# Second-half projections by token block, attention copies on one queue, GpSimd normalising twelve tiles, and a new bank order, in a fused attention and gated-linear block

## The chip, the cores and the metric

The kernel runs on one core of one Trainium2 chip. The metric is device time in microseconds (us), lower is better. Engine names in the profile: PE is TensorE (PEld its weight loads), DVE is VectorE, ACT is ScalarE, POOL is GpSimd, SP is SyncE; a "q" after the name is that engine's instruction queue when it issues DMAs.

## The reference

For 2048 tokens of width 640, in bfloat16:

```python
xn = layernorm(x)                                   # no scale, no bias
q, k, v = split(xn @ wqkv)                          # 32 heads of 20
logits[s, w] = q[s] . k[s - 2*w] * 20**-0.5         # w = 0..7, masked where s - 2*w < 0
attn = softmax(logits) ; o[s] = sum_w attn[s, w] * v[s - 2*w]
h = (xn @ w_gate) * (xn @ w_up)                     # width 1536
out = x + o @ wo + h @ w_down
```

## The kernel before

A small scheduler records every operation in program order, finds its dependencies and emits the semaphore waits. Each engine runs its own operations in the order in which they were recorded, so an operation placed behind a late one is late too.

Layer norm works by tile of 128 tokens, 16 tiles. DVE makes statistics, ACT takes the square root of the variance, DVE inverts it and normalises. Tiles 0 to 3 are transposed by PE; tiles 4 to 15 by a DMA issued from SP.

```python
op("dve", lambda e: e.reciprocal(rstd, sd), r=[("sd", t)], w=[("rstd", t)], name=f"rstd{t}")
op("dve", lambda e: e.tensor_scalar(xs, x, mv[:, 0:1], rstd, op0=ALU.subtract, op1=ALU.mult),
   r=[x, mv, ("rstd", t)], w=[xs], name=f"lnap{t}")
if t >= NTP:                                        # NTP = 4
    op("sp", lambda e: e.dma_start_transpose(o, xs), r=[xs], w=[o], dma=True, name=f"xT{t}")
```

Q and K of the first 1024 tokens are projected while the layer norm runs. Then GpSimd copies the last 14 columns of K's first half in front of its second half (the seam), and the second half's projections begin, in blocks of 512 tokens (`j`): block 2 is tiles 8 to 11, block 3 is tiles 12 to 15.

```python
def k_seam():
    op("pool", lambda e: e.tensor_copy(o, i), r=[i], w=[o], name="kseam")
# ... cut ...
for i, (m, j, which) in enumerate([(m, j, which) for m in range(NCH) for j in (2, 3) for which in (0, 1)]):
    fill.append((1.08, lambda which=which, m=m, j=j: proj(which, m, j)))
# ... cut: then V, gate/up groups and down/out groups, woven with DVE's attention steps
```

Each projection group is five matmuls into one PSUM bank, which ACT evicts; six banks rotate here. DVE forms the logit products in SBUF (q times shifted k), does most of the softmax and the weighted sum of v. The attention weights are spread over partitions by 16 DMAs for each half of the tokens:

```python
for q in range(NSB):
    for r in range(4):
        dma(dst, src, ..., eng=("sp", "act")[r % 2], group=("atb", h))
```

## Time and profile before

| | before |
|---|---|
| time at the start | 267.09 us, median of 3 (266.22 to 267.16) |
| profiled span | 265.8 us |
| PE busy | 256.7 us, 97% |
| DVE busy | 215.7 us, 81% |
| GpSimd busy | 5.3 us |
| PE's granted clock | full throughout, in this execution |

The share of busy time does not tell what a change is worth; PE's waits do. These are lines of the timeline of the kernel before, PE only: start, length, engine, line, operation, count, and in brackets the idle time ahead of the piece and what ended it. The last line is from a later stretch.

```profile
15.95 4.38 PE L436 MATMUL PS<-XNT,WQKV 128*128 128x128 bf16 x75 [0.48 <-ACT KH L450]
20.17 11.08 PE L443 MATMUL PS<-XNT,WQKV 128*128 128x256 bf16 x100
31.09 2.32 PE L423 MATMUL PS<-XNT,WQKV 128*128 128x512 bf16 x10
35.20 1.06 PE L423 MATMUL PS<-XNT,WQKV 128*128 128x512 bf16 x4 [1.79 <-DMA XNT<-XNS]
...
103.68 1.25 PE L576 MATMUL PS<-XNT,WG 128*128 128x512 bf16 x5 [3.26 <-ACT HT L578]
```

PE loses 0.48 us to a bank, 1.8 us to the transpose of tile 15, and 3.3 us to an eviction. The last one has its cause on ACT, of which these are timeline lines:

```profile
93.98 9.00 ACTq L283 DMA_DIRECT2D ATB<-LOG  x8
103.03 0.60 ACT L578 ACTIVATE HT<-PS 128x512 bf16<-128x512 f32 x1 [8.45 <-issue]
```

ACT's queue spends 9.0 us on issuing eight attention copies, and evicts nothing meanwhile; PE runs out of banks.

DVE's own load in the layer norm, one tile's worth, and the seam copy beside the first product (timeline, DVE and POOL; the "waits for" of the copy's 31 us is only its being early):

```profile
30.46 0.45 DVE L370 TENSOR_SCALAR XNS<-XST,MV,SD 128x640 bf16<-128x640 bf16 x1
...
33.91 3.36 DVE L466 TENSOR_TENSOR SL<-QH,KH 128x6144 f16<-128x6144 bf16 x1 [1.36 <-ACT KH L450]
33.94 3.43 POOL L454 COPY KH<-KH 128x70 bf16<-128x70 bf16 x1 [31.45 <-ACT KH L450]
```

A copy of 70 elements a partition takes 3.43 us beside a DVE product of 3.36 us.

### The profile page before, as it was taken

The numbers are of one execution on the slowest core, as the hardware profiler recorded it, in microseconds if no ns is written. First come the engines' busy times: TensorE is split into PE (matmuls) and PEld (weight loads), VectorE is DVE, ScalarE is ACT, GpSimd is POOL, SyncE is SP. The second block draws the span as 40 slices with busy tenths as digits, with TensorE's granted clock in tenths as the row PEclk, the third lists the DMA queues.
The fourth block names the chain that finished last, engine by engine and source line by source line (L and its number), as shares of the span: only waits on it lengthen the run. The fifth ranks groups of instructions, "written<-read, shape, count | busy, mean of one in ns | idle before, by whom it ended". The sixth has DMA issues, their size and how long they took to land.

```text
span 265.8 us, 4020 instructions
## 1 busy us (share of the span) xinstructions
PE 256.7 (97%) x1669; PEld 151.2 (57%) x1669; DVE 215.7 (81%) x240; ACT 106.1 (40%) x193; POOL 5.3 (2%) x13
## 2 busy tenths in 40 slices
PE   8999979999999995999999999999999999999996
PEld 3899835455554442444457754446774444777775
DVE  5799889999985992999997897999999999722211
ACT  3565557555557514655560004752003555100000
POOL 2000050000000000000000000000000000000000
PEclk9999999999999999999999999999999999999999
DMA  6959689200000078009101189100113000031301
GB/s 197 322 131 148 122 257 403 83 2 0 0 0 2 0 157 232 3 7 357 57 0 49 52 175 206 36 2 0 49 52 100 0 0 2 4 94 52 99 27 49
DMA packets 21922, 23.46 MB, mean 88 GB/s; under 512 B 9872, under 2 KB 19472, under 8 KB 21904
## 3 DMA queue, kind: packets, MB, share of 16 engines
q1 hardware_dynamic: 20992, 20.95, 27.7%
q10 hardware_dynamic: 912, 2.26, 4.1%
q8 instruction: 13, 0.21, 0.3%
q14 instruction: 5, 0.04, 0.0%
HBM read 14.42 MB, written 2.62 MB: 64 GB/s over the span
## 4 chain that ended last, share of the span: by engine, by line
PE 82%; DVE 8%; ACTq 3%; DMA 3%; SPq 2%; issue 1%; ACT 1%
PE PS L576 37%; PE PS L607 28%; PE PS L423 16%; ACTq L283 3%; DVE XNS L370 2%; PE PS L484 2%; SPq L283 2%; DVE STATS L354 2%; DMA XST<-in_A_x_dram 2%; DVE STATS L348 2%; DMA XNT<-XNS 1%; DVE MV L360 1%; DVE SD L369 1%; ACT HT L578 0%; ACT USX L578 0%
## 5 line engine op out<-in xcount | busy, mean ns | idle before, releaser
L576 PE MATMUL PS<-XNT,WG 128*128 128x512 bf16 x240 | 59.7, 379 | 3.3 <-ACT HT L578 3.3
L576 PE MATMUL PS<-XNT,WU 128*128 128x512 bf16 x240 | 59.6, 379 | 0.0
L607 PE MATMUL PS<-WD,HT 128*128 128x320 bf16 (+1 forms) x396 | 57.6, 295 | 0.0
L578 ACT ACTIVATE HT<-PS 128x512 bf16<-128x512 f32 x48 | 29.1, 606 | 68.0 <-PE PS L576 34.5
L607 PEld LDWEIGHTS PS<-WD,HT 128*128 128x128 bf16 x396 | 38.1, 98 | 14.7
L423 PE MATMUL PS<-XNT,WQKV 128*128 128x512 bf16 x200 | 43.9, 379 | 1.8 <-DMA XNT<-XNS 1.8
L550 DVE TENSOR_TENSOR PVB<-VO,ATB 128x10240 f16<-128x10240 bf16 x8 | 43.9, 5486 | 0.1
L576 PEld LDWEIGHTS PS<-XNT,WG 128*128 128x128 bf16 x240 | 23.3, 98 | 31.7 <-ACT HT L578 3.8
L576 PEld LDWEIGHTS PS<-XNT,WU 128*128 128x128 bf16 x240 | 23.4, 98 | 28.5 <-issue 0.4
L611 DVE TENSOR_TENSOR FOUT<-PS,XR 128x320 bf16<-128x320 f32 (+1 forms) x33 | 15.5, 476 | 29.1 <-PE PS L607 29.1
L578 ACT ACTIVATE USX<-PS 128x512 bf16<-128x512 f32 x48 | 29.0, 605 | 17.7 <-PE PS L576 17.2
L423 PEld LDWEIGHTS PS<-XNT,WQKV 128*128 128x128 bf16 x200 | 23.3, 118 | 22.0 <-DMA XNT<-XNS 2.3
L545 DVE TENSOR_TENSOR PVB<-PVB 128x5120 f16<-128x5120 f16 (+1 forms) x16 | 34.4, 2148 | 0.0
L466 DVE TENSOR_TENSOR SL<-QH,KH 128x6144 f16<-128x6144 bf16 x8 | 26.8, 3352 | 1.4 <-ACT KH L450 1.4
L581 DVE TENSOR_TENSOR HT<-HT,USX 128x512 bf16<-128x512 bf16 x48 | 18.7, 416 | 10.9 <-ACT USX L578 10.9
L607 PE MATMUL PS<-WO,VO 128*128 128x320 bf16 (+1 forms) x165 | 27.1, 295 | 0.0
L607 PEld LDWEIGHTS PS<-WO,VO 128*128 128x128 bf16 x165 | 15.9, 98 | 5.9
L474 DVE TENSOR_TENSOR SL<-SL,TMP 128x4096 f16<-128x4096 f16 x8 | 18.3, 2289 | 0.2
L466 DVE TENSOR_TENSOR TMP<-QH,KH 128x4096 f16<-128x4096 bf16 x8 | 18.4, 2300 | 0.0
L429 ACT ACTIVATE VO<-PS 128x512 bf16<-128x512 f32 x20 | 11.9, 597 | 9.8 <-PE PS L423 9.8
L436 PE MATMUL PS<-XNT,WQKV 128*128 128x128 bf16 x200 | 12.7, 220 | 0.7 <-ACT KH L450 0.5
L436 PEld LDWEIGHTS PS<-XNT,WQKV 128*128 128x128 bf16 x200 | 11.6, 118 | 1.9 <-ACT KH L450 0.6
(49 smaller groups left out, 138.0 us busy)
## 6 DMA issues: line engine op xcount, KB each, us to landing
XR<-in_A_x_dram SPq DMA_DIRECT2D x16, 160.0 KB, 2.3
XST<-in_A_x_dram SPq DMA_DIRECT2D x15, 160.0 KB, 4.0
out_dram<-FOUT SPq DMA_DIRECT2D x15, 160.0 KB, 1.8
ATB<-LOG SPq DMA_DIRECT2D x16, 128.0 KB, 4.9
ATB<-LOG ACTq DMA_DIRECT2D x16, 128.0 KB, 5.0
WG<-in_B_w_gate_dram SPq DMA_DIRECT2D x1, 1920.0 KB, 9.9
WU<-in_B_w_up_dram SPq DMA_DIRECT2D x1, 1920.0 KB, 14.1
WD<-in_B_w_down_dram SPq DMA_DIRECT2D x1, 1920.0 KB, 8.3
```

The lines of the kernel that those rows point to most:

```text
L283: return op(eng, lambda e: e.dma_start(o, i), r=r, w=w, dma=True, name=name, group=group)
L423: op("pe", (lambda l, x, c: lambda e: e.matmul(PS[:, b, :], l, x, start=(c == 0), stop=(c == NCH - 1)))(l, x, c), r=[l, x], w=[PS[:, b, :] ...
L436: op("pe", (lambda o, l, x, st, sp: lambda e: e.matmul(o, l, x, start=st, stop=sp))(o, l, x, st, sp), r=[l, x], w=[o], name=f"pp{which}_{m ...
L466: return lambda: op("dve", lambda e: e.tensor_tensor(o[:], qw, kw, ALU.mult), r=[q, k], w=[o[:]], name=f"prod{h}_{p}_{c0}")
L474: lambda: op("dve", lambda e: e.tensor_tensor(a, a, b, ALU.add), r=[a, b], w=[a], name=f"psum{h}_{p}")),
L545: return lambda: op("dve", lambda e: e.tensor_tensor(o, x, y, ALU.add), r=[x, y], w=[o], name=f"{name}_{b}")
L550: lambda: op("dve", lambda e: e.tensor_tensor(PVB[:], vw, aw, ALU.mult), r=[v, a], w=[PVB[:]], name=f"pv_{b}")),
L576: op("pe", (lambda l, x, c: lambda e: e.matmul(PS[:, b, :], l, x, start=(c == 0), stop=(c == NCH - 1)))(l, x, c), r=[l, x], w=[PS[:, b, :] ...
L578: op("act", lambda e: e.activation(o, PS[:, b, :], ACT.Copy), r=[PS[:, b, :]], w=[o], name=f"guev{which}_{m}_{j}")
L581: h_pending.append(lambda: op("dve", lambda e: e.tensor_tensor(h, h, o, ALU.mult), r=[h, o], w=[h], name=f"h{m}_{j}"))
L607: op("pe", (lambda l, x, i, b: lambda e: e.matmul(PS[:, b, 0:wid], l, x, start=(i == 0), stop=(i == n - 1)))(l, x, i, b), r=[l, x], w=[PS[ ...
L611: op("dve", (lambda o, xr, b: lambda e: e.tensor_tensor(o, PS[:, b, 0:wid], xr, ALU.add))(o, xr, b), r=[PS[:, b, :], xr], w=[o], name=f"fi ...
```

## The change

The intent: ask for the late tiles later, keep DMA issues off ACT, remove the bank wait, and take 0.45 us a tile off DVE by letting GpSimd normalise. The core of the diff:

```diff
-        op("dve", lambda e: e.tensor_scalar(xs, x, mv[:, 0:1], rstd, op0=ALU.subtract, op1=ALU.mult),
+        op("dve" if t < NTP else "pool",
+           lambda e: e.tensor_scalar(xs, x, mv[:, 0:1], rstd, op0=ALU.subtract, op1=ALU.mult),
 ...
-        for q in range(NSB):
-            for r in range(4):
+        for r in range(4):
+            for q in range(NSB):
                 src, dst = LOG[h][32 * q:32 * q + 32], ATB[h][r:128:4, q]
-                dma(dst, src, ..., eng=("sp", "act")[r % 2], group=("atb", h))
+                dma(dst, src, ..., group=("atb", h))
 ...
-    h_keep = [1]
+    h_keep = [3]
 ...
+        if t0 == 2:
+            bank_ring[:] = [5, 6, 0, 7, 2, 3, 4, 1]
 ...
-    bank_ring[:0] = [6, 7]
 ...
-[(m, j, which) for m in range(NCH) for j in (2, 3) for which in (0, 1)]
+[(m, j, which) for j in (2, 3) for m in range(NCH) for which in (0, 1)]
```

Cut here: the place where the loads of the down and out weights are recorded, and two start constants of the weaving (PE 30.6 to 31.0, DVE 31.5 to 31.8).

More of the change, by code (lines that the diff above doesn't have):

```diff
@@ L529, in attn_move @@
     def attn_move(h):
-        for q in range(NSB):
-            for r in range(4):
+        for r in range(4):
+            for q in range(NSB):
                 src, dst = LOG[h][32 * q:32 * q + 32], ATB[h][r:128:4, q]
-                dma(dst, src, r=[src], w=[dst], name=f"atb{h}_{q}_{r}", eng=("sp", "act")[r % 2], group=("atb", h))
+                dma(dst, src, r=[src], w=[dst], name=f"atb{h}_{q}_{r}", group=("atb", h))
     def pv_steps(b):
@@ L699, in exp_preload @@
         op("act", lambda e: e.activation(DUM[:, 0:1], EPSC[:, 0:1], ACT.Exp), r=[EPSC[:]], w=[DUM[:]], name="exp_preload")
-    t_pe, t_dve = [30.6], [31.5]
+    t_pe, t_dve = [31.0], [31.8]
     fill, pos = [], [0]
@@ L704, in build_kernel @@
     batches = []
-    for i, (m, j, which) in enumerate([(m, j, which) for m in range(NCH) for j in (2, 3) for which in (0, 1)]):
+    loaded = []
+    for i, (m, j, which) in enumerate([(m, j, which) for j in (2, 3) for m in range(NCH) for which in (0, 1)]):
         fill.append((1.08, lambda which=which, m=m, j=j: proj(which, m, j)))
@@ L738, in take @@
         t_pe[0] = max(t_pe[0], at) + 0.44 + 0.2175 * NKC * len(batch)
+        if h == 1 and batch[-1][0] == 3:
+            down_loads()
+            out_loads()
+            loaded.append(True)
     def run_fill(until, upto=None):
@@ L746, in run_fill @@
             if it[0] == "dn":
-                if pv_done[0] <= it[1]:
+                if pv_done[0] <= it[1] or not loaded:
                     return
@@ L813, in build_kernel @@
     settle()
-    down_loads()
-    out_loads()
     for it in headB:
```

## The prediction

> What bounds it now. The page gives TensorE (PE) 97% busy and 82% of the chain that ended last. In the timeline, second-half PE work runs back to back: 40 projection groups and 96 gate/up groups start every 1.08 us, 32 down/out groups every 2.31 us, four logit batches cost about 1.5 us each. That sums to about 227 us, and it occupies 31.1 to 263.5 us (232.4 us): about 5.4 us is stall, in two gaps. VectorE (DVE, 81%) finishes its last attention step at 230 us, well ahead of PE.
>
> The stalls (timeline):
> 1. At 33.2 us PE waits 1.95 us for the transpose of token tile 15. Layer norm on DVE runs 1.65 us a tile, its last normalise ends at 32.6 us, and a transpose lands 2.7 us after issue. The old order needs it in the third group.
> 2. At 100.3 us PE waits 3.4 us. ScalarE's queue issues eight attention copies for 9.0 us, so evictions stop and the PSUM banks run out.
> 3. At 15.5 us PE waits 0.48 us for a bank: tile 3's first projection group takes the bank of the previous pair's mixed group before it is evicted.
>
> What the change does.
> - Token-block order: tiles 12 to 15 are needed only after ten groups (10.8 us), so about 41 us; stall 1 goes: -1.95 us.
> - All 32 copies on SyncE: no DMA issue on ScalarE; stall 2 goes: -3.4 us. Sixteen copies at 0.86 us take about 14 us of SyncE, plus 5 us to land; with row-outer order the first quarter is complete only with copy 13. The DVE has two logit pairs (16 us) and several gate products before it reads them, so this should just fit.
> - Bank order: removes stall 3, at most -0.48 us.
> - GpSimd normalises 12 tiles: DVE loses 0.45 us a tile, its chain falls to about 1.2 us a tile, so ScalarE's evictions no longer wait for late variances and the first logit product should start near 31.5 us instead of 33.9. The Trainium skill, GPSIMD Engine Reference, section 3.1, gives 1.03 cycles an element for short bodies at 1.2 GHz; my estimate from it is 0.7 to 1.3 us for 640 elements. No run shows it yet. The same page says GpSimd shares its SBUF interface with DVE instructions that read two SBUF inputs; this trace agrees: the 70-element seam copy took 3.43 us beside a 3.36 us DVE product. In the layer norm DVE runs one-input operations, so I expect no blocking there. Tile 5 may land about 0.5 us later, which could eat the gain of the bank order.
> - Three gate products kept back: fewer DVE waits for up evictions (10.9 us now); PE hardly gains. Down-weight loads: no effect.
>
> Sum: -5.0 to -5.9 us on a PE-bound chain, minus small new waits. Predicted 261.6 us, 8 in 10 between 260.4 and 263.2. Chances: faster by over 2% 0.52, within 2% 0.45, slower 0.03.
>
> What would show it right: no PE gap near 33 us and 100 us; no DMA issue on ScalarE after start; GpSimd normalises at 0.7 to 1.3 us; second-half projections starting at 30.6 to 31.1 us; span about 260 us.
>
> What would make it wrong: GpSimd above about 1.6 us a tile, so tile 11 or the seam copy comes late and, once DVE products start, is blocked behind them; ScalarE held by the seam copy until PE runs out of banks; attention copies so late on one queue that the products lag and down/out groups wait; delayed gate products blocking an up eviction.

## The result, and the profile after

| | before | after |
|---|---|---|
| time, same rounds | 267.12 us, median of 4 (266.22 to 268.76) | 285.83 us, median of 4 (285.56 to 286.69) |
| ratio of fast runs | | 1.070, 95% interval 1.064 to 1.076 |
| span | 265.8 us | 285.0 us |
| GpSimd busy | 5.3 us | 48.1 us |
| mean granted clock of PE | 1.00 | 0.964 |

Here and below a ratio is the mean time of one kernel's fast runs over that of the kernel before in the same rounds, so it is not quite the ratio of the medians quoted.

The change is 7% slower. First the page's line for the new GpSimd work in the changed kernel (busy us, mean ns of one, idle before it), and that operation's own view (shortest, median, longest in ns):

```profile
L371 POOL TENSOR_SCALAR XNS<-XST,MV,SD 128x640 bf16<-128x640 bf16 x12 | 45.7, 3825 | 10.9 <-DVE SD L369 10.9
```

```profile
L371 POOL TENSOR_SCALAR XNS<-XST,MV,SD x12: 2499/2500/8206, 13.4 to 50.9; 128x640 bf16<-128x640 bf16 x12
```

The median is 2.50 us, and the longest 8.2 us. DVE did the same operation in 0.45 us. Now PE in the changed kernel (timeline), the counterpart of the lines of before:

```profile
21.47 12.78 PE L444 MATMUL PS<-XNT,WQKV 128*128 128x256 bf16 x100 [2.23 <-DMA XNT<-XNS]
36.27 7.50 PE L424 MATMUL PS<-XNT,WQKV 128*128 128x512 bf16 x34 [2.03 <-issue]
60.51 5.87 PE L424 MATMUL PS<-XNT,WQKV 128*128 128x512 bf16 x14 [16.73 <-ACT KH L430]
```

Three new waits stand there. The first, 2.23 us, is for the transpose of an early tile. The second is labelled "issue", but the times say what it is: twelve operations run back to back from 13.43 us, so the eighth, which is tile 11, ends at 13.43 + 8 x 2.485 = 33.3 us, and its transpose lands about 2.7 us later, at 36.0 us, which is when PE begins with block 2. The third is 16.7 us for an eviction into K. The view of ACT's waits, the DVE and POOL timelines of that stretch, and the operation on GpSimd that ended it:

```profile
ACT KH L430 <- POOL KH L455: 21.9, 1, 21.9
```

```profile
34.91 3.36 DVE L467 TENSOR_TENSOR SL<-QH,KH 128x6144 f16<-128x6144 bf16 x1 [3.75 <-ACT KH L451]
38.19 2.28 DVE L467 TENSOR_TENSOR TMP<-QH,KH 128x4096 f16<-128x4096 bf16 x1
40.51 2.77 DVE L475 TENSOR_TENSOR SL<-SL,TMP 128x4096 f16<-128x4096 f16 x1
...
35.77 7.00 POOL L371 TENSOR_SCALAR XNS<-XST,MV,SD 128x640 bf16<-128x640 bf16 x1
42.75 8.21 POOL L371 TENSOR_SCALAR XNS<-XST,MV,SD 128x640 bf16<-128x640 bf16 x1
50.94 8.20 POOL L371 TENSOR_SCALAR XNS<-XST,MV,SD 128x640 bf16<-128x640 bf16 x1
59.10 0.66 POOL L455 COPY KH<-KH 128x70 bf16<-128x70 bf16 x1
```

ACT waited 21.9 us for the seam copy, which stood on GpSimd's queue behind the normalises of tiles 13, 14 and 15. Those three took 7.0, 8.2 and 8.2 us, because DVE's products had begun. One DVE round of two products and a sum takes 8.2 us, and exactly one normalise ends in each round. Since ACT is in order, it could not evict anything, and PE, which had filled its six banks, stopped from 43.8 to 60.5 us.

Then PE's clock. Lines of the table by stretch of the changed kernel (stretch in us, length, busy time and count of PE, PEld, DVE, ACT, POOL, granted clock, DMA share, GB/s):

```profile
60.00:62.00 2.00, 1.50 (x4) 0.60 (x5) 0.00 (x0) 1.98 (x5) 0.00 (x0) 0.50 0.58 96
64.00:66.00 2.00, 2.00 (x7) 0.65 (x5) 0.00 (x0) 1.49 (x3) 0.00 (x0) 0.51 1.04 402
66.00:68.00 2.00, 1.95 (x10) 1.11 (x10) 0.00 (x0) 0.89 (x2) 0.00 (x0) 1.00 1.02 404
```

After the long stop PE runs at half clock until about 66 us. The Trainium skill, page "TensorE: Matmul & The Clock Gate", Part 1, says that PE falls to half clock after an idle window of about 3.4 us and returns after about as long a busy one. This trace agrees that a stop costs more than its length: PE worked at half clock from 60.5 to 65.9 us, which is, as my estimate, 2.7 us lost. It does not agree on the idle time that this takes: the clock had also halved from 21.6 to 24.8 us, after a wait of only 2.23 us.

Where the time went, by the start of each stage in the two timelines:

| stage begins | before | after | later by |
|---|---|---|---|
| second-half projections | 31.09 | 36.27 | 5.2 |
| gate/up groups | 79.31 | 101.88 | 22.6 |
| down/out groups | 137.58 | 156.71 | 19.1 |
| last addition | 263.52 | 282.64 | 19.1 |

The 5.2 us came from the late tiles up to 11: block 2 begins when tile 11 has landed, so the first wait and a clock halved from 21.6 to 24.8 us after it only ate time in which PE would have waited anyway. (In the seam-on-ScalarE run below the clock stayed full there, and block 2 still begins at 36.34 us.) In the next stage 17.4 us came: the 16.7 us stop and about 2.7 us of half clock, less the 1.8 us wait that the new order did remove. The stage after gives back 3.5 us, the wait behind ACT's DMA issues. From there on nothing changes.

### The profile page after: what moved, and what is told of

The parts are those of the page before. It is cut to its first block, busy times and chain, and to the rows that moved or that the text cites. A ratio compares the mean times of both kernels' runs of the same rounds, so it can differ in the third digit from the quotient of the medians.

```text
span 285.0 us, 4001 instructions
## 1 busy us (share of the span) xinstructions
PE 259.1 (91%) x1652; PEld 152.0 (53%) x1669; DVE 212.2 (74%) x228; ACT 108.3 (38%) x193; POOL 48.1 (17%) x25
## 4 chain that ended last, share of the span: by engine, by line
PE 79%; POOL 8%; issue 6%; DMA 3%; SPq 2%; DVE 2%; ACT 1%; ACTq 0%
PE PS L577 36%; PE PS L608 26%; PE PS L424 13%; POOL XNS L371 8%; SPq L283 2%; PE PS L485 2%; DMA XST<-in_A_x_dram 1%; PE PS L444 1%; DMA XNT<-XNS 1%; DVE STATS L354 0%; DVE STATS L348 0%; ACT LOG L492 0%; DVE MV L360 0%; POOL KH L455 0%; ACT KH L430 0%
## 5 line engine op out<-in xcount | busy, mean ns | idle before, releaser
L424 PE MATMUL PS<-XNT,WQKV 128*128 128x512 bf16 x195 | 45.9, 395 | 19.1 <-ACT KH L430 16.7
L577 PE MATMUL PS<-XNT,WG 128*128 128x512 bf16 x231 | 57.7, 379 | 0.6 <-ACT LOG L492 0.2
L371 POOL TENSOR_SCALAR XNS<-XST,MV,SD 128x640 bf16<-128x640 bf16 x12 | 45.7, 3825 | 10.9 <-DVE SD L369 10.9
L424 PEld LDWEIGHTS PS<-XNT,WQKV 128*128 128x128 bf16 x200 | 23.6, 120 | 41.2 <-ACT KH L430 17.2
L475 DVE TENSOR_TENSOR SL<-SL,TMP 128x4096 f16<-128x4096 f16 x8 | 19.6, 2448 | 0.2
L430 ACT ACTIVATE KH<-PS 128x512 bf16<-128x512 f32 x10 | 6.0, 596 | 25.4 <-POOL KH L455 21.9
```

What stands on the lines that cost most here:

```text
L424: op("pe", (lambda l, x, c: lambda e: e.matmul(PS[:, b, :], l, x, start=(c == 0), stop=(c == NCH - 1)))(l, x, c), r=[l, x], w=[PS[:, b, :] ...
L430: op("act", lambda e: e.activation(o, PS[:, b, :], ACT.Copy), r=[PS[:, b, :]], w=[o], name=f"pev{which}_{m}_{j}")
L475: lambda: op("dve", lambda e: e.tensor_tensor(a, a, b, ALU.add), r=[a, b], w=[a], name=f"psum{h}_{p}")),
L577: op("pe", (lambda l, x, c: lambda e: e.matmul(PS[:, b, :], l, x, start=(c == 0), stop=(c == NCH - 1)))(l, x, c), r=[l, x], w=[PS[:, b, :] ...
```

## The experiments

Theory A: all of the loss comes from the GpSimd normalise, its 2.50 us and its slowing beside DVE products, and the rest of the change gains about what was predicted. Rivals: another part of the change costs as well; the seam copy's place on the queue is the real cause; any use of GpSimd beside DVE costs. Twelve kernels ran; the results were correct except in two.

One thing about the kernel before must be known to read the ratios. In the rounds of these experiments 25 of its 36 executions had a mean granted clock of 0.993 or 0.994, and 11 had a full clock, as in the profile above; the medians of the two groups lie 1.2 to 2.1 us apart in the same rounds. The bank-order run below, which keeps the long stop behind ACT's DMA issues, has a trace with such a clock. Its table by stretch shows about 3.4 us of half clock right after that stop, which is, as my estimate, 1.7 us lost:

```profile
104.00:106.00 2.00, 2.00 (x7) 0.76 (x6) 1.46 (x2) 1.98 (x5) 0.00 (x0) 0.59 0.60 202
106.00:108.00 2.00, 2.00 (x6) 0.69 (x5) 2.00 (x3) 0.60 (x1) 0.00 (x0) 0.56 0.03 8
```

All 22 executions of the four kernels below that have neither that stop nor a long early wait (all tiles on DVE, copies only, four late tiles, half width late) had a full clock. So part of a ratio can be clock, and where it matters the times at equal clock are given too. No trace of the kernel before itself with the lower clock was kept.

### All tiles on DVE

```diff
-        op("dve" if t < NTP else "pool",
+        op("dve",
```

> The change with only the GpSimd normalise undone (VectorE normalises all tiles). Theory A (the whole loss comes from GpSimd: 2.50 us a tile, one after another, and the last ones stretched to 7 to 8 us beside VectorE products): 260.5 to 262.5 us, no PE gap at 33 us or at 100 us, 0.976 to 0.983 of the kernel before. Rival B (one of the other parts, the single copy queue, the held-back gate products or the new order, costs too): over 265 us.

Measured: 262.25 us (262.0 to 262.6), ratio 0.979, interval 0.975 to 0.983. The gaps at 33 and 100 us are gone, clock full. So the other parts together gain 2.1% (the interval reaches both sides of a 2% gain), close to the 2.0% to 2.2% that the prediction gave them, and rival B falls. That it is so close is partly luck: against the five full-clock runs of the kernel before in these rounds (median 266.97 us) the gain is 4.7 us, 1.8%, and the rest is the clock drop, which the prediction did not contain.

### GpSimd alone

The kernel before, with only the normalise of tiles 4 to 15 moved:

```diff
-        op("dve", lambda e: e.tensor_scalar(xs, x, mv[:, 0:1], rstd,
+        op("dve" if t < NTP else "pool",
+           lambda e: e.tensor_scalar(xs, x, mv[:, 0:1], rstd,
```

> The kernel before with only the GpSimd normalise added. Theory A: worse than the full change, 290 to 300 us, because the old order asks for tile 15 in the third projection group and tile 15 lands at about 62 us. Rival B (the loss needs the other parts): 265 to 275 us.

Measured: 295.86 us, ratio 1.104. A line of PE's timeline of this kernel:

```profile
62.11 2.33 PE L424 MATMUL PS<-XNT,WQKV 128*128 128x512 bf16 x5 [23.53 <-DMA XNT<-XNS]
```

In the old order tile 15 is asked for in the third group, so PE stands 23.5 us. The normalise alone is enough for the loss, and the token-block order softened it.

### The seam copy on ScalarE

```diff
-        op("pool", lambda e: e.tensor_copy(o, i), r=[i], w=[o], name="kseam")
+        op("act", lambda e: e.activation(o, i, ACT.Copy), r=[i], w=[o], name="kseam")
```

> The change with the seam copy moved from GpSimd to ScalarE, so that ScalarE's K eviction no longer waits behind the queue of normalises. Theory A (the tiles themselves are late, the seam copy is only one way in which this reaches PE): PE does the ten groups of the third token block and then waits for tile 15's transpose until about 62 us; 280 to 286 us. Rival C (the seam copy at the end of the GpSimd queue is the cause, token-block order leaves enough slack for the tiles): the 16.7 us gap goes and the time is 264 to 270 us.

Measured: 283.36 us, ratio 1.060. PE's timeline of this kernel:

```profile
36.34 10.96 PE L424 MATMUL PS<-XNT,WQKV 128*128 128x512 bf16 x50 [3.34 <-DMA XNT<-XNS]
61.22 5.13 PE L424 MATMUL PS<-XNT,WQKV 128*128 128x512 bf16 x14 [13.92 <-DMA XNT<-XNS]
```

PE now does all ten groups of block 2 (50 matmuls) and then waits 13.9 us for a transpose. The seam copy was the wait that ended last in the changed kernel, but taking it away wins only 2.5 us (and the intervals, 1.053 to 1.068 here and 1.064 to 1.076 for the full change, overlap), because the tiles are as late. Following one chain of waits shows one path; here two ran side by side.

### Even tiles only

```diff
-        op("dve" if t < NTP else "pool",
+        op("dve" if t < NTP or t % 2 else "pool",
```

> The change with GpSimd normalising only the even tiles from 4 on (6 tiles), VectorE the odd ones. Theory A (what matters is that 2.5 us a tile exceeds the pace of 1.2 us at which VectorE hands tiles over): two tiles now take VectorE about 2.85 us, GpSimd keeps up with 2.5 us, is done by about 31 us, before the first product; 260 to 262.5 us. Rival D (any GpSimd normalise beside VectorE slows VectorE or delays tiles): over 264 us.

Measured: 263.64 us (263.5 to 266.1), ratio 0.987, interval 0.982 to 0.992. This is above the range of theory A and below that of rival D, and 1.4 us more than with all tiles on DVE in the same rounds. All six operations took 2.50 us and were done by 33.3 us, so nothing was stretched; but PE waited 2.54 us at 21.6 us for an early tile. GpSimd keeps up, yet tile 4 passes through it 2.05 us slower than through DVE (2.50 against 0.45 us), and tiles 4 and 5 have no such slack.

### The other parts one at a time, on the kernel before

Token-block order only:

> The kernel before with only the token-block order of the second half's projections. As predicted: the 1.95 us gap at 33 us goes and VectorE, which waits for PE's first up eviction, moves forward with it, so the gain survives to the end: ratio 0.991 to 0.995. Rival: the gap at 100 us ends at a time set by ScalarE's queue, grows by as much, and the gain is lost: 0.997 to 1.003.

Measured: 266.84 us, ratio 0.9935, interval 0.990 to 0.9975. As predicted a gain survives: at equal clock it is 1.4 us in both groups (265.0 us against 266.4 at full clock, two runs each, and 267.0 against 268.4). The profile's span is 2.6 us shorter than that of the profile above, but that one is from other rounds. The wait near 100 us was 2.8 us instead of 3.3.

Attention copies only (SP, row outer, quarter inner):

> The kernel before with only the attention copies changed (all on SyncE, row outer, quarter inner). As predicted: the 3.4 us gap at 100 us goes, nothing waits for the copies: ratio 0.985 to 0.989. Rival: sixteen copies on one queue finish late, the first product of the weights waits, and part of the gain is given back: 0.990 to 1.0.

Measured: 263.67 us, ratio 0.983, interval 0.980 to 0.986, so slightly below the expected 0.985 to 0.989. The gap is gone. The clock was full in all six runs; against the two full-clock runs of the kernel before in these rounds (266.3 and 266.4 us) the gain is 2.7 us, and the rest of the 4.4 us in the ratio is the clock drop that goes with the gap. (The span is 3.6 us shorter than that of the profile above, from other rounds.) The sixteen copies are issued faster than I had estimated, 10.2 us instead of 14, and land sooner, 2.6 us instead of 5. First the issue list's lines of the kernel before (size of each, median us to landing), then those of this kernel and its SP timeline:

```profile
ATB<-LOG SPq DMA_DIRECT2D x16, 128.0 KB, 4.9
ATB<-LOG ACTq DMA_DIRECT2D x16, 128.0 KB, 5.0
```

```profile
ATB<-LOG SPq DMA_DIRECT2D x32, 128.0 KB, 2.6
...
93.00 10.15 SPq L283 DMA_DIRECT2D ATB<-LOG  x16
```

On two queues eight copies took 6.85 us on SP beside 9.0 us on ACT, so one queue is 0.63 us a copy where two were 0.86 on SP and 1.12 on ACT. The Trainium skill, page "DMA: Bandwidth & Descriptors", section "Issuing engines are not separate DMA queues", says that issuing from several engines only saves the sequencer's issue time; here it saved next to nothing even of that: sixteen were issued within 9.8 us on two queues (93.2 to 103.0 us) and within 10.2 us on one. Whether the row-outer order has a part in it was not tried apart.

Bank order only:

> The kernel before with only the bank order. The 0.48 us gap at 15.5 us goes, but PE then waits 0.5 us longer at 33 us, because tile 15 comes from VectorE at the same time: ratio 0.998 to 1.002. Rival (the prediction's sum, in which it adds up): 0.9975 or less, 0.5 us earlier at the end.

Measured: 268.50 us, ratio 1.001, interval 0.996 to 1.005 (one slow run left out). At full clock it took 266.5 us, the kernel before 266.3 and 266.4. The bank wait went, and PE's wait for tile 15 grew from 1.8 to 2.3 us in its trace. In my prediction's sum the two savings were added; alone, this one shows no gain. That PE only arrives earlier at the same late tile is likely but not shown: tile 15 also landed 0.7 us earlier in this trace than in that of the kernel before, which is from other rounds.

### GpSimd on four late tiles

```diff
-        op("dve" if t < NTP else "pool",
+        op("pool" if t in (8, 10, 12, 14) else "dve",
```

> The change with GpSimd normalising only tiles 8, 10, 12 and 14 (four operations of 2.5 us with at least 2.8 us between them), VectorE the others, so that no tile on the early deadline (4 to 7) is slowed as in the even-tile run, where PE waited 2.5 us at 21 us. Theory A: GpSimd is done before the first product, PE has no wait for a transpose over 0.5 us, the first product starts near 32 us instead of 33.5, and the 0.6 us wait of the logits at 49 us goes: 261 to 262 us, ratio 0.972 to 0.979. Rival D (any GpSimd normalise costs): 262.5 us or more.

Measured: 260.99 us (260.6 to 262.0), ratio 0.974, interval 0.971 to 0.977. This beats both kernels: 2.6% faster than before. How much of that is GpSimd's is not shown: the kernel with all tiles on DVE, run in other rounds, had 0.979 (0.975 to 0.983), and the intervals overlap; at full clock the two gained 5.4 and 4.7 us on the kernel before. Its GpSimd timeline, and one line of DVE's:

```profile
19.81 2.50 POOL L371 TENSOR_SCALAR XNS<-XST,MV,SD 128x640 bf16<-128x640 bf16 x1 [17.32 <-DVE SD L369]
22.65 2.50 POOL L371 TENSOR_SCALAR XNS<-XST,MV,SD 128x640 bf16<-128x640 bf16 x1 [0.34 <-DVE SD L369]
26.60 2.50 POOL L371 TENSOR_SCALAR XNS<-XST,MV,SD 128x640 bf16<-128x640 bf16 x1 [1.44 <-DVE SD L369]
29.41 2.50 POOL L371 TENSOR_SCALAR XNS<-XST,MV,SD 128x640 bf16<-128x640 bf16 x1 [0.31 <-DVE SD L369]
...
24.35 0.98 DVE L371 TENSOR_SCALAR XNS<-XST,MV,SD 128x640 bf16<-128x640 bf16 x1 [0.67 <-DMA XNT<-XNS]
```

GpSimd waits for DVE before each one, never the reverse, and is done at 31.9 us, ahead of the first product at 32.3 us. The view of PE's waits lists none after the start. One of DVE's own normalises, begun while GpSimd was at work, took 0.98 us instead of 0.45; the other eleven took 0.45. So GpSimd beside DVE's layer norm costs PE nothing when it keeps the pace, and rival D falls.

### What the operation costs

The all-DVE kernel with a row of GpSimd operations on scratch data, once beside the layer norm and again after the last attention step:

```python
e.tensor_scalar(dst, src, c0, c1, op0=ALU.subtract, op1=ALU.mult)    # 640 columns, and 320
e.tensor_scalar(dst, src, 0.5, 2.0, op0=ALU.subtract, op1=ALU.mult)  # immediates
e.tensor_scalar(dst, src, 0.5, None, op0=ALU.mult)                   # one step
e.tensor_scalar(f32, f32, c0, c1, op0=ALU.subtract, op1=ALU.mult)    # 32-bit
e.tensor_copy(dst, src)
```

> The kernel with VectorE normalising all tiles, plus a row of GpSimd operations on scratch data, once beside the layer norm and once after the last attention step, when VectorE is nearly idle (results are not used). If the 2.50 us are the operation's own cost: the two-step bfloat16 operation on 640 columns takes 2.4 to 2.6 us at both places, and about half on 320 columns. Rival (VectorE's one-input statistics hold GpSimd's port): 2.5 us beside the layer norm and 0.7 to 1.3 us, my estimate, at the end. The immediate-operand, one-step, 32-bit and plain-copy forms show which part of the form costs; I expect the copy below 1 us.

The probe's GpSimd timeline, beside the layer norm:

```profile
12.72 2.50 POOL L336 TENSOR_SCALAR PDST<-PSRC,PC 128x640 bf16<-128x640 bf16 x1
15.32 1.43 POOL L337 TENSOR_SCALAR PDST<-PSRC,PC 128x320 bf16<-128x320 bf16 x1
16.84 2.35 POOL L338 TENSOR_SCALAR PDST<-PSRC 128x640 bf16<-128x640 bf16 x1
19.28 1.82 POOL L339 TENSOR_SCALAR PDST<-PSRC 128x640 bf16<-128x640 bf16 x1
21.09 2.56 POOL L340 TENSOR_SCALAR PF<-PF,PC 128x640 f32<-128x640 f32 x1
23.60 0.71 POOL L341 COPY PDST<-PSRC 128x640 bf16<-128x640 bf16 x1
```

After 233 us, with DVE nearly idle, the same row took 2.51, 1.43, 2.35, 1.82, 2.51 and 0.72 us. So the 2.50 us are the operation's own, and DVE's statistics do not slow it. (DVE's own normalises were slowed: three of sixteen took 0.66 to 0.82 us instead of 0.45 while the probe ran.) From 320 to 640 columns it grows by 1.07 us, which is 3.3 ns a column on a fixed 0.36 us. Immediates save 0.15 us, dropping one step another 0.53, and the type hardly matters (2.56 and 2.51 us in 32 bits); only the plain copy is fast. (The kernel's own time, 271.44 us from one run, says nothing: the probe reads a buffer of token tile 4, so the next token load waited for it until 24.3 us, and PE waited 7.9 us for a transpose.)

### Half the width

The full change, but GpSimd normalises 320 of the 640 columns, and the others are left as they are. Its output is wrong, which doesn't matter for the time.

```diff
+        hw = D if t < NTP else DHALF
-           lambda e: e.tensor_scalar(xs, x, mv[:, 0:1], rstd, op0=ALU.subtract, op1=ALU.mult),
+           lambda e: e.tensor_scalar(xs[:, 0:hw], x[:, 0:hw], mv[:, 0:1], rstd, op0=ALU.subtract, op1=ALU.mult),
```

> Wrong result on purpose: the full change, but GpSimd normalises only the first 320 of 640 columns of tiles 4 to 15, so that its operation takes about what I had estimated (near 1.3 us if the cost goes with the columns). Everything else, order, queues and waits, is the full change. Theory A (only the size of this one term was wrong): no gap at 42 to 60 us, the prediction's mechanism holds, 260.4 to 262.5 us. Rival (a queue of twelve operations on GpSimd with the seam copy behind it is harmful whatever their size): over 265 us.

Measured: 265.03 us (262.9 to 265.4), ratio 0.986, interval 0.981 to 0.991. The operations took 1.44 us, a little above the top of my estimate, and the gap at 42 to 60 us is gone; so the sign of the result turns with the size of this term. But the time is above the range, and just over the line where I had put the rival. A line of PE's timeline, and the time to landing of the two transposes issued up to 16.7 us, tiles 4 and 5 (shortest, median, longest):

```profile
21.27 12.78 PE L445 MATMUL PS<-XNT,WQKV 128*128 128x256 bf16 x100 [2.05 <-DMA XNT<-XNS]
...
DMA to landing us min/median/max: 2.7/3.6/4.5
```

Tile 5's transpose was issued at 16.69 us and took 4.5 us, so it came at 21.2 us, when PE had been ready for two microseconds. PE then ran on a halved clock from 21.4 to 24.8 us; three of the four runs had a mean clock of 0.994, and the one with a full clock took 262.9 us. So even at my estimated size the early tiles would have cost about 2 us and some clock, where I had allowed 0.5.

### Half the width, early tiles on DVE

The same, with tiles 4 to 7 whole on DVE; also wrong. In the diff above, `t < NTP` becomes `t < 8` in both places.

> Wrong result on purpose: as the half-width run, but tiles 4 to 7 are normalised whole on VectorE; GpSimd does 320 columns of tiles 8 to 15 (1.44 us each). The half-width run lost 2.0 us at 21 us to tile 5, whose transpose came 4.5 us after its issue, and then ran on a halved clock to 25 us. If that early deadline is all that kept it from the prediction: no PE wait for a transpose over 0.5 us, second half from 30 to 31 us, 260.5 to 262.3 us. Rival (something else in the GpSimd queue costs too): over 263 us.

Measured: 261.26 us, ratio 0.974, interval 0.971 to 0.978; second-half projections from 30.55 us, no PE wait for a transpose, and the first DVE product at 31.16 us. With about the size that I had assumed (1.44 us, where my estimate ended at 1.3), eight tiles instead of twelve and the early deadline met, the prediction's mechanism and its time hold. No other cost of the queue shows. Nor does a gain from GpSimd show clear of noise: the all-DVE kernel's 0.979 (0.975 to 0.983) overlaps.

### Full width, early tiles on DVE

```diff
-        op("dve" if t < NTP else "pool",
+        op("dve" if t < 8 else "pool",
```

> The full change, but tiles 4 to 7 normalised on VectorE; GpSimd does tiles 8 to 15 whole (8 operations of 2.50 us, correct result). Theory: what costs most is the number of normalises still queued when VectorE's products start, and eight from about 19.5 us on, after DVE's first products near 32 us, leave three, as twelve from 13.4 us did; so the early tiles being on time helps little: the gap near 40 to 58 us stays, 279 to 285 us. Rival (the slow start of the first tiles is what costs): under 270 us.

Measured: 282.64 us, ratio 1.053. PE waited 17.1 us for K's eviction (16.7 us in the full change), and the longest normalise took 8.2 us again. Fewer operations help little (1.053 against 1.070) if they begin later and some still stand on the queue when the products start; it is the tail beside the products that costs most.

## Why the prediction was wrong, point by point

- **What bounds the kernel.** Right. PE's stalls were named by place and size, and the kernel with all tiles on DVE removed them: ratio 0.979.
- **"-1.95 us" for the token order.** Held within the noise: 0.9935 alone, 1.4 us at equal clock. **"-3.4 us" for the copies.** The wait went; at full clock it was worth 2.7 us, and 4.4 us in the ratio, because the stop also cost clock in most executions. The issue time was mis-sized, 14 us estimated and 10.2 measured, to no effect.
- **Bank order "at most -0.48 us".** Alone it shows no gain (1.001, 0.996 to 1.005).
- **The step that failed: "my estimate from it is 0.7 to 1.3 us for 640 elements".** It measured 2.50 us, twice the top of the estimate. The Trainium skill, page "GPSIMD Engine Reference", section 3.1, gives 1.03 cycles an element for short bodies, and section 4.1 calls one-input work roughly line-rate. That fits the plain copy here (0.71 us) and not the normalise: 3.3 ns a column is, as my estimate with the page's 1.2 GHz, about 4 cycles. The measurement decides. I had no duration in the trace for this operation and took a rate for short bodies as one for this instruction. So the relief of DVE did not arrive either: the first logit product was expected near 31.5 us instead of 33.9 and began at 34.91.
- **What follows from it was foreseen, but rated too low.** The text names both consequences under what would make it wrong: "GpSimd above about 1.6 us a tile", and then blocking behind DVE products. Both happened: three normalises took 7.0 to 8.2 us. I gave slower a chance of 0.03, with a term in the sum that no trace had shown.
- **"Tile 5 may land about 0.5 us later".** Too small. In the half-width run PE waited 2.05 us for it and lost clock, since its transpose took 4.5 us to land, where I had used the median of 2.7.
- **"I expect no blocking there"** (beside the layer norm). Right for GpSimd: the probe shows equal durations beside DVE's statistics and without them. Not quite for DVE, some of whose normalises took up to 0.98 us instead of 0.45 beside GpSimd.
- **The clock was not in the prediction at all.** It made the long stop dearer by an estimated 2.7 us, and it was already in the kernel before: most executions lost about 1.7 us after the stop near 100 us, which the profiled one did not show.

What stays open: why one normalise ends in each DVE round. It ends at 42.75 us, 2.2 us into the sum (40.51 to 43.28), so it looks as if the two products with broadcast inputs hold GpSimd and the sum lets it through, but no run separated them. The rule is not simply "blocked while a product runs": tile 12's normalise, which had 0.9 us to go when the first product began, still took 2.50 us, and the seam copy of the kernel before ended at 37.37 us, 0.1 us after the first product and not in a sum. The held-back gate products and the place of the weight loads were not tried apart either; the all-DVE kernel, which has both, shows no harm.

## What to carry to other kernels

Before moving work to another engine, measure that very instruction there, in the form in which it will run; a rate for a simpler one can be off by two or more. An engine that another one can slow has a deadline: here GpSimd's normalises had to be over before DVE's first product, and those left on its queue then took three times as long and held up everything behind them. Give such an engine only what it can do at the pace of its feeder, and begin with the items that have slack. Measured against the kernel before, everything else of the change included, four of twelve tiles gave 2.6%, none 2.1%, six 1.3%, and twelve lost 7%: twelve and six were worse than none, and that four are better than none is not clear of noise. And one profile may miss what most executions do: compare runs at the same granted clock.

## What the Trainium skill lacked or had wrong

- "GPSIMD Engine Reference", sections 3.1 and 4.1: short bodies are given 1.03 cycles an element, and one-input work is called roughly line-rate. A tensor-scalar operation on 128x640 took 2.50 us with two steps and pointer scalars, 2.35 us with immediates and 1.82 us with one step; only the copy (0.71 us) fits.
- The same page, section 1 (contention with DVE instructions in a 2-port mode or with two SBUF inputs): this page gives no size. The skill has more on it in its page on SBUF, which was not used here. Here a 2.50 us operation took 7.0 to 8.2 us beside DVE products, a 70-element copy 3.43 us beside a product of 3.36 us, and DVE's sum went from 2.29 us to between 2.69 and 2.77 us. A DVE normalise beside a GpSimd one took up to 0.98 us instead of 0.45.
- "DMA: Bandwidth & Descriptors", section "Issuing engines are not separate DMA queues": it does not say whether issuing from two queues at once slows each of them. Sixteen 128 KB copies took 10.2 us of issue and 2.6 us to land on one queue; on two, 0.86 and 1.12 us each to issue and 5 us to land (the order of the copies differed too).
- The same page, for DMA transposes: the time to landing was mostly 2.6 to 2.8 us and up to 5.0 us (tile 6 of the four-late-tiles run, issued at 17.5 us); it gives rates, not this spread, and no run here shows its cause.
- "TensorE: Matmul & The Clock Gate", Part 1: it gives an idle window of about 3.4 us before the half clock. Here waits of 2.23 us (changed kernel) and 2.05 us (half width) were followed by it, while waits of 2.52 us (seam on ScalarE) and 2.54 us (even tiles) were not in the traces kept. After the stops of 7.9 to 23.5 us the half clock lasted 3.8 to 5.4 us of work; as the page lets its window run freely, that is not against its 3.4 us.
